# Attention and a four-expert mixture in one kernel: row loads held by GpSimd copies, one mask tile, a gate ring of two, and a refitted order

## The chip, the cores and the metric

The kernel runs on one core of a Trainium2 chip. A core has a matrix engine (TensorE, PE in the profile; its weight loads are shown apart as PEld), a vector engine (VectorE, DVE), an activation engine (ScalarE, ACT), GpSimd (POOL) and a sync engine (SyncE, SP) that here only issues DMAs. GpSimd too issues DMAs. Engines run their own queues in order and wait for each other by semaphores. The metric is the device time of one execution in microseconds, as the median of several runs.

## What is computed

Four batches of attention with 8 heads, 768 positions and head size 64. Each position sees the first 4 positions (the sinks) and the last 128 (the window). The result is laid out as 3072 tokens of 512 features and goes through four experts, each two matrix products with a ReLU between; the experts' outputs are summed with weights that are normalised per token.

```python
keep = is_sink | in_window                       # first 4 keys, or 0 <= q-k < 128
a = softmax(where(keep, q @ k.T / 8, -1e9))
x = (a @ v)                                      # as (3072, 512)
p = domain_probs / (domain_probs.sum(-1) + 1e-9)
out = sum_e p[:, e] * (relu(x @ w1[e]) @ w2[e])  # w1: 512x1024, w2: 1024x512
```

## The kernel before

Tokens are taken in pairs of 128-row blocks: three pairs in each of four batches, named (b, g). Attention of a batch makes the rows x of its three pairs; the mixture turns each pair, for each expert e, into a "unit" (b, g, e): first layer, ReLU and gate, second layer.

**Attention.** q and k rows come as tiles `qkn` by cast loads on GpSimd's DMA queue (`load_nat`, L248), v as `vx` (`load_v`, L316). For batch 0 TensorE turns them (L605), for the later ones SP issues a DMA transpose into `qkT` (`turn_nat`, L259). `scores` (L689) makes products of 64-row tiles (L708), two heads side by side; ScalarE takes the exponential (L733) into `aT`; VectorE multiplies by a 0/1 mask (L727 for both heads of a later batch, L742 for one head of batch 0); in the first group of batch 0 the mask is instead added by a product with `ident` (L702). `values` (L751) multiplies by v (L774, and L767 for the sinks); then normalisation (L801 to L819), and a DMA transpose of `onat` into `xT` (L791). `sinks` (L669) holds the scores of the first four keys, on 32-column tiles. For the sinks of group 1 in a batch from 1 on, all row blocks that they cover must be turned.

**Mixture.** The first layer is either plain (L1118) or "fast": a seven-product scheme on 2x2 blocks (P1 to P7) whose additions VectorE and ScalarE do. Fast units come in two forms. In the gated form (`emit_fast`, L1182; products L1208) VectorE multiplies with a gate row that was spread over all partitions: `gates`, 128 KB per unit, loaded by SP from a DRAM tile `gate_rows` (`load_gate`, L471, DMA L478). In the turned form (`emit_turning`, L1285; products L1320) the token is on the partition, the gate is a column of `own_gates`, and the result X goes through a DMA transpose (L1301) into H; X needs two free half tiles for each unit, kept in the list `resting`. The second layer of most pairs is a chain of seven products (L1493) on H and on sums S0, S1 that VectorE makes (`chore`, L1434 and L1411); of the first two pairs it is plain (L1579) with the gate applied at L1589 and L1591 into `osbw`.

**Order.** The kernel plans itself while it is built. Lines 118 to 229 keep a clock for every engine and for two DMA queues; each recorded instruction advances them by an estimated cost (`act`, `dve`, `pool`, `lands`, `sp`). `later(engine, ready, slack, run)` puts work of VectorE and ScalarE on a list; `flush` records the piece that is due first. The main loop (L1662) records, at each step, the PE work of lowest priority number that is ready (scores, values, a first-layer product, a second-layer product); numbers such as DUE, LEAD, SHARE_OF, FORM and MASK set these priorities. So constants move instructions on every engine. Loads stand in the list `loads` and are recorded when the plan says that their buffer is free; at run time GpSimd issues them in this order as soon as the semaphores allow, which can be earlier or later than planned. `held` (L1703) is a two-element GpSimd copy of `qkT` after the last transposes of batches 1 and 2: GpSimd issues nothing that stands behind it until these have landed.

The gate tiles form a ring of four (`NGATE = 4`): the load for unit n may go when unit n-4 is done.

Of the kernel before, what the change touches and what calls it, by code (L numbers as in the profile page):

```python
# [16 lines left out]
def kernel(  # L17
# [46 lines left out]
    EXPERTS = {(1, 0): (0, 2, 1, 3), (1, 1): (3, 2, 1, 0), (1, 2): (3, 2, 1, 0), (2, 2): (2, 0, 3, 1), (3, 1): (3, 2, 1, 0)}  # L64
# [7 lines left out]
    LOW_SECOND = 2.7  # L72
    HIGH_PRODUCT = 1.9
    EARLY = -0.01
    MASK = 5000
    GATE = 800
    GATE0 = 300
    FORM = 6000
    TOKEN = 3000
    MARGIN = 500  # L80
    HOLD = 0
    FULL = 7
    STEP0 = 0.03
    READY = 40
    REST = 3000
    LANDS = 0
    SCALED = 300
    SHARED = 2
    MARGIN1, MARGIN2 = 4000, 14000
    OWNED_READ = 152  # L90
    WIDE = 2
    OPEN = 2.5
    SOON = 34000
# [6 lines left out]
    ONE = 2  # L100
    HOLDS = 2
    MORE = 2
    BOTH = 1
    PAIR = 0
    OVER = 4
    ALONE = 2.0
    BEHIND = 1500
    CHORES = 3
    BIASED = 1
# [349 lines left out]

    gate_sb = {}  # L460
    gate_tiles = [consts.tile([P, 2, 2, P], FP32, name=f"gates{i}") for i in range(NGATE // 2)]

# [8 lines left out]
    def load_gate(pair, e):  # L471

        i = len(gate_sb) % NGATE
        x = gate_tiles[i // 2][:, i % 2]
        if FIRST <= len(gate_sb) < NGATE:
            nc.vector.memset(x[0:1, 0, 0:1], 0.0)
            dve(1, fixed=150)
        nc.sync.dma_start(  # L478
            out=x.rearrange("p t n -> p (t n)"), in_=gate_rows[pair, e].rearrange("t n -> (t n)").partition_broadcast(P),
        )  # L480
        gate_sb[pair, e] = x
        sp(takes=300)

# [26 lines left out]
    for tb in (2, 3):  # L510
# [18 lines left out]
    LOW = 32768.0  # L529
    low = [lent[:, 5 * P:8 * P], lent[:, 8 * P:12 * P]]  # L530
    nc.vector.tensor_scalar(
        out=low[0].rearrange("p (n q) -> p n q", n=3)[:, 0::2], in0=two, scalar1=LOW, scalar2=-LOW, op0=ALU.mult, op1=ALU.add,
    )
    nc.vector.tensor_scalar(out=low[0][:, P:2 * P], in0=own, scalar1=-LOW, scalar2=None, op0=ALU.mult)
    nc.vector.memset(low[0][0:NSINK, 0:2 * P], 0.0)
# [3 lines left out]
    x = low[1].rearrange("p (n c q) -> p n c q", n=2, c=2)  # L539
    nc.scalar.activation(out=x[:, :, 0], in_=two, func=AF.Copy, scale=-LOW)  # L540
    nc.scalar.activation(out=x[:, :, 1], in_=two, func=AF.Copy, scale=LOW, bias=-LOW)
    mask0 = consts.tile([P, 3 * P], BF16, name="mask0")
    mask1 = consts.tile([P, 4 * P], BF16, name="mask1")
    made = []

    def make_mask(i):
        def run(engine):
            x = (mask0, mask1)[i]
            if i:
                nc.scalar.activation(out=x, in_=low[i], func=AF.Copy, scale=1 / LOW, bias=1.0)  # L550
                act(4 * P)
            else:
                nc.vector.tensor_scalar(out=x, in0=low[i], scalar1=1 / LOW, scalar2=1.0, op0=ALU.mult, op1=ALU.add)
                dve(3 * P)
            made.append(i)
        later(("dve", "act")[i], (24000.0, 11700.0)[i], 8000, run)
# [132 lines left out]
    def scores(b, hp, g, more=False):  # L689
# [10 lines left out]
        if biased:  # L700
            for ph in range(2):
                nc.tensor.matmul(sps[ph][:, 0:w], lhsT=ident, rhs=low[min(g, 1)], start=True, stop=False, skip_group_check=True)  # L702
            pe(2 * w, ready, n=2)
# [18 lines left out]
        if b == 0:  # L722
            part = join(2, masked)
        else:
            def mask_both(at):
                def run(engine):
                    nc.vector.tensor_mul(a, a, m[:, None, :].to_broadcast([P, 2, w]))  # L727
                    masked(dve(2 * w, rate=1.92))
                later("dve", at, MASK, run)
            part = join(2, mask_both)  # L730
        for ph in range(2):
            def run(engine, ph=ph):
# [8 lines left out]
                def mask_one(engine):  # L741
                    nc.vector.tensor_mul(a[:, ph], a[:, ph], m)  # L742
                    part(dve(w, rate=1.92))
# [216 lines left out]
    class Mixture:  # L960


        def __init__(self):
# [13 lines left out]
            mine = [u for u in self.order if u[0] >= OWN]  # L977
            self.turning = set(mine[TURNED_UNITS[0]:len(mine) - TURNED_UNITS[1]])
# [46 lines left out]
        def opened(self, b, g, e):  # L1025
# [11 lines left out]
            def complete(at):  # L1037
                self.H_at[b, g, e] = at
                self.finished.add((b, g, e))
                if (b, g) >= PAIRS[0]:  # L1040
                    self.waiting.append((b, g, e))
                    load_gates()
                    if not TURNED_UNITS[1] and self.gated[-1] == (b, g, e):
                        self.rest_gates()
# [39 lines left out]
        def emit_first(self, what, ready):  # L1084
# [56 lines left out]
            def run(engine):  # L1141
# [5 lines left out]
                part(at)  # L1147
            later("dve", end, GATE0, run)

# [32 lines left out]
        def emit_fast(self, u, m, ready):  # L1182
# [40 lines left out]
            def gated(dst, src, half_, ready, slack, slot=None, then=None):  # L1223
# [16 lines left out]
                def run(engine):  # L1240
# [44 lines left out]
        def emit_turning(self, u, m, ready):  # L1285
# [47 lines left out]
            def gated(k, s, src, ready, slack, slot=None, then=None):  # L1333
                gate = own_gates[:, 2 * ((b - OWN) * NG + g) + s, e:e + 1]

                def run(engine):
                    if engine == "act":
                        nc.scalar.activation(out=src, in_=src, func=AF.Relu)  # L1338

                        def scaled(engine):  # L1340
                            nc.scalar.mul(X[k][:, :, s], src, gate)  # L1341
                            done(act(n))
# [3 lines left out]
                    done(dve(n, fixed=OWNED_READ))  # L1346

                def done(at):
                    if slot is not None:
                        take(slot, at)  # L1350
# [40 lines left out]
        def chore(self):  # L1391
# [40 lines left out]
            def form(engine):  # L1432
                x = steps.pop(0)
                x[0](*x[1:])  # L1434
                at = dve(QF * P, self.stored[-1] if (b, g) == PAIRS[0] else 0.0, rate=1.92)
                if steps:
                    go(form, self.until(b, g, e, "P6 P7".split()[len(steps) == 2]))
# [128 lines left out]
        def emit_second(self):  # L1566
# [20 lines left out]
            def run(engine):  # L1587
                if e == 0:
                    nc.vector.tensor_scalar(out=dst, in0=op, scalar1=sc, scalar2=None, op0=ALU.mult)  # L1589
                else:  # L1590
                    nc.vector.scalar_tensor_tensor(  # L1591
                        out=dst, in0=op, scalar=sc, in1=dst, op0=ALU.mult, op1=ALU.add,
                    )
# [5 lines left out]
            later("dve", end, 400, run)  # L1599
            self.since = 0  # L1600
# [36 lines left out]
    work = [sum(NFB * NDB * G * (1 if (b, g) < START[e] else 7 / 8) + NFB * NDB * G * (1 if (b, g) < PAIRS[0] else 7 / 8) for g in range(NG) for e in range(E)) for b in range(B)]  # L1637
    ahead, upto, loaded, wide, rowed = 0, 0.0, 0, 0, 0
    asked = []
# [22 lines left out]
    while mix.more() or att.more():  # L1662
# [28 lines left out]
        if x and t["pool"] < now + 1500 and free_ring(x):  # L1691
            loads.remove(x)
            x[0](*x[1:])
        if turns and (ahead < 2 or not mix.second) and landed.get(("qk", *turns[0]), 1e12) < now and (turns[0][0] <= ahead or turns[0][0] == ahead + 1 and not att.todo):
# [7 lines left out]
            if 0 < b < B - 1 and x[1] == NQB - 1:  # L1702
                nc.gpsimd.tensor_copy(out=held, in_=qkT[b][:, 1, NHP - 1, S - 2:S])  # L1703
                pool(2, turned_at[x])
                nat_loads(b + 1, range(NQB))
                turns += [(b + 1, tb) for tb in range(NQB)]
        flush(now)
        mix.tokens()
# [3 lines left out]
        if ahead + 1 < B and not att.more() and (ahead == 0 or (ahead + 1, 0) in turned_at) and (ahead == 0 or mix.done >= sum(work[:ahead]) * LEAD[ahead - 1]):  # L1712
            ahead += 1
            if ahead == 1:
                own_load()
            elif ahead == 2:
                own_made()
            att = Attention(ahead)
# [79 lines left out]
```

## Time and profile before

| what | value |
|---|---|
| median of 3 runs | 354.05 us (353.97 to 354.15) |
| span of the profiled execution | 351.9 us |
| first matmul / start of the last | 1.4 us / 348.5 us |
| PE, PEld, DVE, ACT, POOL busy | 346.2, 266.0, 282.8, 208.3, 71.6 us |
| matmuls | 3721 |
| granted TensorE clock | 1.000 |
| gate loads (L478) | 20 of 128 KB |
| DMA transposes | 67 |

The profile gives the profiled execution by its span, from its first instruction to its last; the runs' time is 2.15 us longer. Times inside the profile count from the start of the span. The chain of waits is followed back from the last instruction: each piece says what the next one had to wait for. A matmul's duration contains its way through the array, so its pace is read from many in a row. In the stage table the two numbers after a stage are its length and PE's busy time; the number behind x is a count.

### The profile page before, as it was taken

How to read it: one execution, taken by the hardware profiler on the slowest of the kernel's cores; microseconds unless marked ns; L12 is line 12 of the kernel's file. 1: busy time of each engine (PE TensorE's matmuls, PEld its weight loads, DVE VectorE, ACT ScalarE, POOL GpSimd, SP SyncE). 2: the span in 40 equal slices, each digit the busy share in tenths (PEclk: the TensorE clock that was granted, in tenths of full speed). 3: DMA queues.
4: the chain of work that ended last, by engine and by line, in shares of the span. 5: the costliest groups of instructions: out<-in, count | busy, mean ns of one | idle time of the engine just before them, and what ended most of it. 6: DMA issues, size and time to landing. Idle time of an engine off the chain costs nothing.

```text
span 351.9 us, 9351 instructions
## 1 busy us (share of the span) xinstructions
PE 346.2 (98%) x3721; PEld 266.0 (76%) x3721; DVE 282.8 (80%) x672; ACT 208.3 (59%) x476; POOL 71.6 (20%) x89
## 2 busy tenths in 40 slices
PE   8999999999999999999999999999999999999996
PEld 3685769656789998998999886755856676666685
DVE  5886999878999999799898999578768586675740
ACT  6863624447874443647453539689589767666611
POOL 8946114330546206100152000000000000000000
PEclk9999999999999999999999999999999999999999
DMA  9999999999999999920999602545437733545441
GB/s 178 178 188 195 223 214 181 179 160 174 162 147 165 121 145 122 132 64 9 109 173 159 113 32 62 120 101 120 80 91 174 127 89 93 120 120 115 67 120 61
DMA packets 161032, 45.61 MB, mean 130 GB/s; under 512 B 144740, under 2 KB 156996, under 8 KB 160988
## 3 DMA queue, kind: packets, MB, share of 16 engines
q0 software_dynamic: 79104, 17.31, 56.4%
q1 hardware_dynamic: 80828, 27.18, 40.1%
q8 instruction: 29, 0.48, 0.5%
q10 hardware_dynamic: 1056, 0.52, 0.5%
q14 instruction: 15, 0.12, 0.1%
HBM read 38.39 MB, written 6.34 MB: 127 GB/s over the span
## 4 chain that ended last, share of the span: by engine, by line
PE 75%; DMA 19%; POOL 5%; issue 1%; ACT 0%; POOLq 0%; SPq 0%
PE acc L1493 35%; PE cps L1320 17%; PE cps L1208 15%; DMA w<-in_moe_w_dram 12%; DMA qkn<-in_k_dram 4%; DMA qkT<-qkn 3%; PE sps L708 3%; PE od L774 2%; POOL qkn L251 2%; POOL w L331 1%; POOL vx L318 1%; PE hps L1118 1%; PE od L767 1%; POOL w L341 0%; PE acc L1579 0%
## 5 line engine op out<-in xcount | busy, mean ns | idle before, releaser
L1493 PEld LDWEIGHTS <-H 128*128 128x128 bf16 x708 | 66.5, 98 | 17.9 <-issue 1.1
L1493 PE MATMUL acc<-w,H 128*128 128x256 bf16 x420 | 56.9, 273 | 0.0
L733 ACT ACTIVATE aT<-sps 128x512 bf16<-128x512 f32 (+1 forms) x96 | 47.2, 579 | 16.3 <-PE sps L708 16.2
L1208 PEld LDWEIGHTS <-w 128*128 128x128 bf16 x640 | 39.1, 98 | 1.2 <-issue 0.5
L1493 PEld LDWEIGHTS <-S 128*128 128x128 bf16 x320 | 30.3, 98 | 9.5 <-issue 0.8
L1241 DVE SCALAR_TENSOR_TENSOR H<-cps,gates 128x512 bf16<-128x512 f32 x54 | 36.6, 683 | 0.0
L1338 ACT ACTIVATE cps<-cps 128x512 f32<-128x512 f32 x44 | 25.5, 585 | 17.5 <-PE cps L1320 17.0
L1118 PE MATMUL hps<-xT,w 128*128 128x256 bf16 x256 | 31.9, 273 | 0.1
L819 ACT ACTIVATE onat<-od,R 128x64 bf16<-128x64 f32 x108 | 24.9, 324 | 11.4 <-DVE R L801 11.1
L318 POOL DMA_DIRECT2D vx<-in_v_dram x24 | 21.4, 903 | 43.0 <-PE od L774 31.2
L1208 PEld LDWEIGHTS <-vf 128*128 128x128 bf16 x480 | 29.3, 98 | 1.0 <-issue 0.5
L1579 PE MATMUL acc<-w,H 128*128 128x512 bf16 x128 | 29.9, 379 | 0.0
L1493 PE MATMUL acc<-wf,H 128*128 128x256 bf16 (+1 forms) x216 | 29.6, 272 | 0.0
L1118 PEld LDWEIGHTS <-w 128*128 128x128 bf16 x256 | 24.1, 98 | 4.7 <-issue 0.9
L1341 ACT ACTIVATE rest<-cps,own_gates 128x512 bf16<-128x512 f32 x37 | 25.5, 693 | 0.7
L727 DVE TENSOR_TENSOR aT<-aT,mask 128x1024 bf16<-128x1024 bf16 (+1 forms) x36 | 22.7, 640 | 3.1 <-ACT aT L733 2.8
L251 POOL DMA_DIRECT2D qkn<-in_q_dram x22 | 19.7, 896 | 23.3 <-DMA qkT<-qkn 14.7
L1208 PE MATMUL cps<-T,w 128*128 128x128 bf16 x320 | 24.3, 219 | 0.0
L1208 PE MATMUL cps<-xT,w 128*128 128x128 bf16 x320 | 24.1, 219 | 0.0
L1320 PE MATMUL cps<-w,T 128*128 128x512 bf16 x80 | 23.8, 379 | 0.0
L1320 PE MATMUL cps<-vf,T 128*128 128x512 bf16 x80 | 23.6, 379 | 0.0
L1554 ACT COPY osb<-acc 128x256 f32<-128x256 f32 x32 | 12.1, 382 | 19.3 <-PE acc L1493 19.1
(145 smaller groups left out, 673.5 us busy)
## 6 DMA issues: line engine op xcount, KB each, us to landing
w<-in_moe_w_dram POOLq DMA_DIRECT2D x6, 1024.0 KB, 18.4
out_dram<-osb SPq DMA_DIRECT2D x16, 256.0 KB
vx<-in_v_dram POOLq DMA_DIRECT2D x24, 128.0 KB, 6.5
qkn<-in_q_dram POOLq DMA_DIRECT2D x22, 128.0 KB, 6.7
qkn<-in_k_dram POOLq DMA_DIRECT2D x22, 128.0 KB, 7.4
gates<-gate_rows SPq DMA_DIRECT2D x20, 128.0 KB
w<-in_moe_w_dram POOLq DMA_DIRECT2D x4, 256.0 KB, 6.9
w<-in_moe_w_dram POOLq DMA_DIRECT2D x2, 512.0 KB, 11.5
```

The costliest lines, as they stand in the source:

```text
L251: nc.gpsimd.dma_start(out=both[:, i], in_=src[b, :, tb * P:(tb + 1) * P, :].rearrange("h p d -> p h d"),)
L318: nc.gpsimd.dma_start(out=vx[tb][:, :, 0:D], in_=v[b, :, tb * P:(tb + 1) * P, :].rearrange("h p d -> p h d"),)
L733: nc.scalar.activation(out=a[:, ph], in_=sps[ph][:, 0:w], func=AF.Exp, scale=scale)
L819: nc.scalar.mul(o[:, qi, hp, ph * D:(ph + 1) * D], od[:, qi, ph, 0:D], R[:, qi, ph])
L1118: nc.tensor.matmul(h[:, i].rearrange("p (q n) -> p q n", q=2), lhsT=w1_sb[e][:, db, fb * P:(fb + 1) * P], rhs=xT[b, g][:, :, db], start=(i ...
L1208: nc.tensor.matmul(y[:, f], lhsT=A[:, d, f * P:(f + 1) * P], rhs=T[:, d], start=(m in ("P1", "P5") and f == 0 and d == 0), stop=(d == 1), ...
L1241: nc.vector.scalar_tensor_tensor(out=dst, in0=src, scalar=0.0, in1=gate, op0=ALU.max, op1=ALU.mult)
L1320: nc.tensor.matmul(y.rearrange("p f n -> p (f n)"), lhsT=T[:, d], rhs=A[:, d], start=(m in ("P1", "P5") and d == 0), stop=(d == 1), skip_g ...
L1338: nc.scalar.activation(out=src, in_=src, func=AF.Relu)
L1341: nc.scalar.mul(X[k][:, :, s], src, gate)
L1493: nc.tensor.matmul(y, lhsT=self.operand(b, g, e, m)[:, f], rhs=forms[e][m][:, f, cs], start=(k == 0 and f == 0 and m in (("P1", "P5", "P2" ...
L1579: nc.tensor.matmul(op, lhsT=H[:, fb // QF, fb % QF, s], rhs=w2_sb[e][:, fb, :], start=(fb == 0), stop=(fb == NFB - 1),)
```

## The change

- **Held row loads.** `marked` remembers the tile that VectorE last wrote by plan (a masked `aT`, an X, an S or H sum). Before each recorded q/k or v load of batches 2 and 3 (`HELD = 2`), `hold` has GpSimd copy two elements of that tile into `held`. The load, behind it in GpSimd's queue, can't go earlier. There are 24 such copies, beside the two of before.
- **One mask tile.** `masks` (four 128-column blocks) takes the place of `mask0` (three) and `mask1` (four). The column order of group 0 is changed (`GROUPS[0]`), so that the first group's mask is blocks 1 to 3 and the other groups use blocks 0 and 1 twice by broadcast. The second bias source `low[1]` and its two ScalarE operations are gone.
- **Gate ring of two.** `NGATE = 2`: the load for unit n goes when unit n-2 is done; the plan has a gating wait for `gate_at`, its gate's landing.
- **Turned units.** Two tiles `row0`, `row1` are in `resting` from the start (`HALVES = 2`). The turned units are the same 20 as before, now written out as a list; `own_gates` covers batches 1 to 3 instead of 2 and 3 (72 columns instead of 48), and is normalised 26 us of plan after its load.
- **First pairs' scaling.** The scaling for e = 0 (four of them) goes from VectorE to ScalarE.
- **Costs and constants.** The plan's costs of ScalarE, VectorE and loads are changed, and most of the constants; experts' order within a pair is changed. The built program has the same products; one more dummy matmul stands in the head (26 for 25).

```diff
-        [(0, 0, 2), (1, 1, 1)],
+        [(1, 1, 1), (0, 0, 2)],
...
-    NGATE = 4
+    NGATE = 2
-    OWN = 2
-    TURNED_UNITS = (4, 0)
+    OWN = 1
+    TURNED_UNITS = (0, 0, ..., 1, 1)
-    MIX = 6
-    SHARE_OF = (1.01, 0.92, 0.96)
-    LEAD = (1.01, 0.99)
-    DUE = 1.9
+    MIX = 9
+    SHARE_OF = (0.92, 0.89, 0.95)
+    LEAD = (1.005, 0.97)
+    DUE = 1.6
-    MASK = 5000
-    GATE = 800
-    FORM = 6000
+    MASK = 8500
+    GATE = 300
+    FORM = 3500
-    LANDS = 0
+    LANDS = -1400
+    HALVES = 2
+    HELD = 2
+    GATE_LANDS = 600
...
-        t["act"] = at + max(196, 68 + cols / 1.23)
-        return at + max(350, 205 + cols / 1.2)
+        t["act"] = at + max(200, 76 + cols / 1.23)
+        return at + max(375, 230 + cols / 1.2)
-        t["dve"] = at + fixed - 85 + cols / rate
-        return at + fixed + 35 + cols / rate
+        t["dve"] = at + fixed - 77 + cols / rate
+        return at + fixed + 60 + cols / rate
+    mark = []
+    def marked(at, x):
+        mark[:] = [at, x]
+    def hold():
+        nc.gpsimd.tensor_copy(out=held, in_=mark[1])
+        pool(2, mark[0])
-        at = max(t["sw"], issued + 1500)
+        at = max(t["sw"], issued + 800)
...
         gate_sb[pair, e] = x
-        sp(takes=300)
+        gate_at[pair, e] = sp(takes=300) + GATE_LANDS
...
-            later("dve", end, GATE0, run)
+            later("dve", max(end, gate_at[b * NG + g, e]), GATE0, run)
...
-                later("dve", ready, slack, run)
+                later("dve", max(ready, gate_at[b * NG + g, e]), slack, run)
...
-            self.G, self.resting = {}, []
+            self.G = {}
+            self.resting = [(0.0, mo.tile([P, QF, 2, P], BF16, name=f"row{i}", tag=f"row{i}", bufs=1)) for i in range(HALVES)]
...
                 if e == 0:
-                    nc.vector.tensor_scalar(out=dst, in0=op, scalar1=sc, scalar2=None, op0=ALU.mult)
+                    nc.scalar.mul(dst, op, sc)
...
             loads.remove(x)
+            if x[0] is not load_w1 and x[0] is not load_w2 and x[1] >= HELD:
+                hold()
             x[0](*x[1:])
```

More of the change, by code (lines that the diff above doesn't have):

```diff
@@ L100 @@
     ONE = 2
-    HOLDS = 2
+    HOLDS = 3
     MORE = 2
@@ L104 @@
     PAIR = 0
[L105 to L108, printed above, removed]
+    OVER = 5
+    ALONE = 0.3
+    BEHIND = 2400
+    CHORES = 5
     BIASED = 1
@@ L529 @@
     LOW = 32768.0
-    low = [lent[:, 5 * P:8 * P], lent[:, 8 * P:12 * P]]
+    low = lent[:, 5 * P:8 * P]
     nc.vector.tensor_scalar(
-        out=low[0].rearrange("p (n q) -> p n q", n=3)[:, 0::2], in0=two, scalar1=LOW, scalar2=-LOW, op0=ALU.mult, op1=ALU.add,
+        out=low.rearrange("p (n q) -> p n q", n=3)[:, 0:2], in0=two, scalar1=LOW, scalar2=-LOW, op0=ALU.mult, op1=ALU.add,
     )
-    nc.vector.tensor_scalar(out=low[0][:, P:2 * P], in0=own, scalar1=-LOW, scalar2=None, op0=ALU.mult)
-    nc.vector.memset(low[0][0:NSINK, 0:2 * P], 0.0)
+    nc.vector.tensor_scalar(out=low[:, 2 * P:], in0=own, scalar1=-LOW, scalar2=None, op0=ALU.mult)
+    nc.vector.memset(low[0:NSINK, P:], 0.0)
     nc.vector.reduce_sum(
@@ L538 @@
     )
[L539 to L543, printed above, removed]
+    masks = consts.tile([P, 4 * P], BF16, name="masks")
+    mask0, mask1 = masks[:, P:], masks[:, 0:2 * P]
     made = []
@@ L547, in run @@
         def run(engine):
-            x = (mask0, mask1)[i]
             if i:
-                nc.scalar.activation(out=x, in_=low[i], func=AF.Copy, scale=1 / LOW, bias=1.0)
-                act(4 * P)
-            else:
-                nc.vector.tensor_scalar(out=x, in0=low[i], scalar1=1 / LOW, scalar2=1.0, op0=ALU.mult, op1=ALU.add)
-                dve(3 * P)
+                nc.scalar.activation(out=masks[:, 0:P], in_=own, func=AF.Copy, scale=-1.0, bias=1.0)
+                nc.scalar.copy(out=masks[:, P:2 * P], in_=own)
+                act(P)
+                act(P)
+            else:
+                nc.vector.tensor_scalar(out=masks[:, 2 * P:], in0=low[:, P:], scalar1=1 / LOW, scalar2=1.0, op0=ALU.mult, op1=ALU.add)
+                dve(2 * P)
             made.append(i)
@@ L701, in scores @@
             for ph in range(2):
-                nc.tensor.matmul(sps[ph][:, 0:w], lhsT=ident, rhs=low[min(g, 1)], start=True, stop=False, skip_group_check=True)
+                nc.tensor.matmul(sps[ph][:, 0:w], lhsT=ident, rhs=low, start=True, stop=False, skip_group_check=True)
             pe(2 * w, ready, n=2)
@@ L726, in run @@
                 def run(engine):
-                    nc.vector.tensor_mul(a, a, m[:, None, :].to_broadcast([P, 2, w]))
-                    masked(dve(2 * w, rate=1.92))
+                    x = a if g == 0 else a.rearrange("p h (r c) -> p (h r) c", r=2)
+                    nc.vector.tensor_mul(x, x, m[:, None, :].to_broadcast([P, 2 if g == 0 else 4, w if g == 0 else 2 * P]))
+                    at = dve(2 * w, rate=1.92)
+                    marked(at, a[:, 1, w - 2:w])
+                    masked(at)
                 later("dve", at, MASK, run)
@@ L1042, in complete @@
                     load_gates()
-                    if not TURNED_UNITS[1] and self.gated[-1] == (b, g, e):
+                    if self.gated[-1] == (b, g, e):
                         self.rest_gates()
@@ L1345, in run @@
                     nc.vector.tensor_scalar(out=X[k][:, :, s], in0=src, scalar1=0.0, scalar2=gate, op0=ALU.max, op1=ALU.mult)
-                    done(dve(n, fixed=OWNED_READ))
+                    done(dve(n, fixed=OWNED_READ) if slot is not None else dve(n, rate=1.92, fixed=214))
                 def done(at):
+                    marked(at, X[k][:, 0, s, 0:2])
                     if slot is not None:
@@ L1435, in form @@
                 at = dve(QF * P, self.stored[-1] if (b, g) == PAIRS[0] else 0.0, rate=1.92)
+                marked(at, x[1][:, 0, 0:2])
                 if steps:
@@ L1588, in run @@
                 if e == 0:
-                    nc.vector.tensor_scalar(out=dst, in0=op, scalar1=sc, scalar2=None, op0=ALU.mult)
[L1590 to L1593, printed above, removed]
+                    nc.scalar.mul(dst, op, sc)
+                    acc_free[bank] = act(Dout)
+                    return
+                nc.vector.scalar_tensor_tensor(
+                    out=dst, in0=op, scalar=sc, in1=dst, op0=ALU.mult, op1=ALU.add,
+                )
                 acc_free[bank] = at = dve(Dout, fixed=218)
@@ L1598, in run @@
                     self.stored.append(sp(at))
-            later("dve", end, 400, run)
+            later("dve" if e else "act", end, 400, run)
             self.since = 0
@@ L1637 @@
     work = [sum(NFB * NDB * G * (1 if (b, g) < START[e] else 7 / 8) + NFB * NDB * G * (1 if (b, g) < PAIRS[0] else 7 / 8) for g in range(NG) for e in range(E)) for b in range(B)]
-    ahead, upto, loaded, wide, rowed = 0, 0.0, 0, 0, 0
+    ahead, upto, loaded, wide, rowed, owned = 0, 0.0, 0, 0, 0, 1e12
     asked = []
@@ L1706 @@
                 turns += [(b + 1, tb) for tb in range(NQB)]
+        if owned + OWNS < now:
+            owned = 1e12
+            own_made()
         flush(now)
@@ L1715 @@
                 own_load()
-            elif ahead == 2:
-                own_made()
+                owned = now
             att = Attention(ahead)
```

37 lines of the change are left out of this document (20 added, 17 removed).

## The prediction, as put on record before the changed kernel ran

> **What bounds the kernel now.** I read the page's busy shares, then the chain of waits in order of time, then the stage table, then single rows.
>
> ```profile
> span 351.9 us, 9351 instructions
> PE 346.2 (98%) x3721; PEld 266.0 (76%) x3721; DVE 282.8 (80%) x672; ACT 208.3 (59%) x476; POOL 71.6 (20%) x89
> ...
> PE 75%; DMA 19%; POOL 5%; issue 1%; ACT 0%; POOLq 0%; SPq 0%
> ```
>
> PE is nearly never idle. But a busy PE is not yet a streaming PE, so I take paces from the chain's pieces:
>
> ```profile
> 60.20 14.86 DMA qkn<-in_k_dram
> 75.11 10.75 DMA qkT<-qkn
> ...
> 117.01 2.18 PE acc L1493 x20
> ...
> 200.80 4.91 PE cps L1208 x88
> ```
>
> A 256-column matmul takes 2.18/20 = 0.109 us, a 128-column one 4.91/88 = 0.056. With the 512-column pace (0.216) and the score matmuls counted once per row-group pair, which start 3 ns apart, the 3721 matmuls stream for 334.1 us. The rest of 351.9 is: 1.4 before the first matmul, 3.4 after the start of the last, 31 visits to the row-tiled scores and sinks at 0.19 each (5.9), and waits, about 7. The 0.19 is read at one visit:
>
> ```profile
> 93.40 1.04 PE L1118 MATMUL hps<-xT,w 128*128 128x256 bf16 x8
> 94.37 0.29 PE L669 MATMUL sinks<-qkT,ksd 128*32 128x256 bf16 x4
> 94.59 0.62 PE L708 MATMUL sps<-qkT 64*128 64x128 bf16 x12
> 95.14 0.39 PE L1493 MATMUL acc<-w,H 128*128 128x256 bf16 x2
> ```
>
> The eight matmuls from 93.40 fill 8 x 0.109, to 94.27; the sinks start 0.10 late. The twelve scores stream 0.45 us, to 95.04; the next product starts 0.10 late. Of the 7 us of waits, 1.5 is the half-rate clock of the dummy matmuls before 5 us, which no order changes, and about 4 are data waits before 23 us. After 25 us only 1.17 is left: 0.37 at 86.0 (sinks behind the DMA transposes of the chain above), 0.15 and 0.12 near 241, 0.13 and 0.08 at 140, and four pieces of 0.04 to 0.14. **So PE's own work sets the end, and little idle time is left to win.** VectorE is next:
>
> ```profile
> 100.00:110.00 10.00, 10.00 (x161) 9.30 (x159) 10.00 (x25) 7.31 (x25) 3.39 (x4) 1.00 1.69 161
> 150.00:160.00 10.00, 10.00 (x150) 9.22 (x148) 9.96 (x23) 5.14 (x16) 0.00 (x0) 1.00 0.17 56
> 310.00:320.00 10.00, 10.00 (x71) 6.65 (x69) 5.57 (x13) 6.65 (x13) 0.00 (x0) 1.00 0.61 157
> ```
>
> Columns: stage, PE, PEld, DVE, ACT, POOL, clock, DMA share, GB/s. From 90 to 190 us DVE is busy 76 to 100%: a microsecond that DVE loses there is hard to make up. After 210 it has room.
>
> **The change, part by part.** Places below are PE streaming time, added up at these paces along the built program; another engine's instruction has the place of the PE instruction beside which it was recorded. Place 148.2 of before is 155.56 on the profile's clock: add about 7.
>
> *PE's own list.* The refitted order has 3722 matmuls: one more 256-column dummy in the head (+0.11). Visits to row-tiled matmuls rise from 31 to 34, because pairs of score steps are split more often: 3 x 0.19 = +0.57. Sum **+0.68**, certain, and on the path, since PE is the bound. The Trainium skill (TensorEngine Tiling (Array Packing), Key Properties) says that changing the tiling mode drains TensorE; by that rule each visit must cost, and the 0.10 on each side agrees.
>
> *Batch 1's rows.* From 12 to 86 us the chain is row and weight loads. The ring of two takes two 128 KB gate loads out of it: those issued at 37.80 and 38.28, whose packets took 1.8 us each beside other loads (42.71 to 44.53, 44.49 to 46.41). The wait of 0.37 at 86.0 needs only 0.37 of that. Between 0 and -0.37, I take **-0.3**, nearest to its being gone. Next late is PE itself.
>
> *Head and masks.* The two ScalarE operations of the second mask source (0.42 and 0.40 us at 3.8 to 4.6) go, the mask itself becomes two 128-column copies; VectorE's casts at 5.07 follow its own queue, so nothing moves. Four flips now stand ahead of a turn that waited 0.16 (12.65), and two turns are joined where one waited 0.25 (20.61). Between 0 and -0.41: **-0.15**, in the middle, as the chain through VectorE behind them is unchanged.
>
> *Later waits.* The 0.8 left after 25 us beside the 86.0 one can all go, or be replaced by others: the numbers of recorded steps with under 0.9 us from producer to PE are 31 before and 21 after (places from 30 on), a thinner list. Between -0.8 and +0.5: **-0.3**. In it lies the shift of six gatings from ScalarE (0.59 + 0.69 each) to VectorE (0.75) in the last stage, where DVE has room, and of four scalings of 0.75 from VectorE to ScalarE around 70, where ScalarE is under half busy.
>
> *Gate ring of two.* Before, a gate load was recorded at least 19 us ahead of its first use. Now the load waits until the unit two back is gated, and the 16 later ones lead by 2.0 (place 148.2 to 150.2), 4.1 (91.4), 4.7 (174.4), 5.3 (176.9), 6.3 (117.8), 6.4 (111.9), 7.4 twice, the rest 9 or more. Issue to last packet, from before's 20 gate loads: 2.4 to 3.1 in quiet stretches (152.83 to 155.38, 155.56 to 158.49), 3.8 to 8.1 beside row loads. So at 150 VectorE stops 0.5 to 1.0, at 95 up to 0.6, near 180 up to 1.0, near 124 up to 1.0. Behind that instruction stand all of VectorE's queue; PE's bank releases there have some 0.9 us of lead. PE pays 0 to 1.5 in all: **+0.3**, since the one sure late load exceeds PE's lead by about nothing to 0.4. The Trainium skill (DMA: Bandwidth & Descriptors, Anatomy of one DMA) gives 2.0 us and 0.3 for 128 KB, an estimate of 2.3 for each; by it only the 2.0 lead is short and this term is +0.1; the loads of 3.8 and more beside row loads say that it is a floor.
>
> *Held loads.* 24 copies of 128x2 join POOL's queue ahead of the row loads, each waiting for one VectorE write. The two such copies of before:
>
> ```profile
> POOL held L1703 <- DMA qkT<-qkn: 34.2, 2, 18.8
> ...
> L1703 POOL COPY held<-qkT x2: 184/212/240, 92.0 to 135.0; 128x2 bf16<-128x2 bf16 x2
> ```
>
> 24 x 0.21 = 5 us on an engine with 20% busy: covered. Queued behind each are the row loads, behind these SP's transposes and then the scores. The copies also add waits the other way: whoever next writes the marked tile waits for POOL. The closest are ScalarE's exponentials at places 90.1 and 92.3, 7.4 and 6.3 us after their copies; POOL starts 2 to 3 us late there, as its queue is held by batch 1's transposes to 91.95. Enough cover. Contention is the other cost: 13.20 (POOL, 1.16 us) and 13.99 below.
>
> ```profile
> 13.20 1.16 POOL L647 TENSOR_TENSOR vsd<-vsf,sel 128x520 bf16<-128x520 f32 x1
> 13.99 0.52 DVE L1174 TENSOR_TENSOR T<-xT 128x256 bf16<-128x256 bf16 x1
> ```
>
> That VectorE step takes 0.28 in the median, here 0.52. The two copies at 92.0 and 135.0 lengthened nothing beside them. So each costs VectorE 0 to 0.24, 0 to 5.8 in all, and PE 0 to 0.5: **+0.1**, near the copies' own rows. The Trainium skill (SBUF — State Buffer, the shared port pair) has VectorE's two-input steps and GpSimd's reads exclude each other for a whole instruction; by it about half the copies would block VectorE, an estimate of 2.5 us of its time, and PE's part would be +0.3.
>
> Row loads now start when planned, so fewer run into transposes; their landing is not on the path unless the rival below holds: 0.
>
> **Sum**: +0.68 - 0.3 - 0.15 - 0.3 + 0.3 + 0.1 = +0.33: span 352.2. The runs' median stands 2.15 above the span (354.05 against 351.9); carried over: **354.4**, +0.1%. That counts as no change: 0.2%, 0.71 us, is about what a measurement of this kernel can tell.
>
> **Rivals.** *Batch 2's rows come late (slower).* In before, nine loads from 108.38 to 115.30 and the transposes among them hamper each other:
>
> ```profile
> 118.25 0.32 SPq L478 DMA_DIRECT2D gates<-gate_rows  x1
> ...
> 121.57 12.03 SPq L263 DMA_TRANSPOSE qkT<-qkn  x2
> 133.70 2.20 SPq L478 DMA_DIRECT2D gates<-gate_rows  x3
> ```
>
> The last row load, issued at 115.30, landed at 131.62, and the last transpose at 135.0: 19.7 us. Held loads put the last issue at place 114.9, about 122.3; with the same 19.7 they end at 142.0. Batch 2's sinks stand at place 132.9, 139.9, so PE stops 2.1; the gate loads behind these transposes (place 120.9, used at 128.3) come late too, another 0.5 to 1.5. It decides from a drain of over 17.6 us. For it: nine loads in 7.5 us of places again. Against it: an undisturbed series (92.44 to 100.92) drains in 15, and three transposes now go ahead of the loads. 354.4 + 2.1 + 1 = 357.5; a milder form, in which gate loads alone wait, gives 355.2 to 356.
>
> *The refit pays (faster).* All the wins come and no cost: 0.68 - 0.37 - 0.41 - 0.8 = -0.90, 353.15. Against it: it needs every wait gone.
>
> *The change does nothing*: +0.68 and the waits as they are but for the 86.0 one: 354.4, inside the forecast.
>
> **Chances.** Forecast (within 0.2%) 0.55; gate or row lateness beyond it 0.33, of which the full form 0.1; faster 0.12. The likeliest case's own range is 353.4 to 354.7. Leaving out half of the faster case and the full late form, the range is 353.3 to 355.9.
>
> **What would show it.** The static part: 34 visits and PE's streaming sum +0.68. Gate: VectorE waits for DMA gates near 157 and 102 on the profile's clock. Held loads: last row load of batch 2 issued near 122, landing by 132, and PE's sinks near 140 without a DMA wait. The 86.0 wait gone. I am wrong if PE waits over 1 us after 90, or if VectorE's two-input steps beside the copies are longer by 0.2.

## The result, and the profile after

| kernel | median (range) | runs | before, beside it | ratio, 95% interval |
|---|---|---|---|---|
| changed kernel | 358.88 us (358.45 to 359.25) | 4 | 354.09 | 1.0138 [1.0121, 1.0154] |
| the same, run again | 358.97 us (358.36 to 359.41) | 4 | 353.77 | 1.0143 [1.0128, 1.0158] |

The change makes the kernel 1.4% slower. 354.4 was forecast and 355.9 was the upper end of the range: the prediction was wrong. The profiled execution of the changed kernel took 358.63 us. The page's span, its busy line and its chain by engine:

```profile
span 356.9 us, 9383 instructions
...
PE 348.1 (98%) x3722; PEld 266.2 (75%) x3722; DVE 284.0 (80%) x677; ACT 200.8 (56%) x462; POOL 78.6 (22%) x113
...
PE 60%; DMA 23%; DVE 9%; POOL 5%; issue 2%; ACT 0%; POOLq 0%; DVEq 0%; SPq 0%
```

PE's busy share is 98% as before, and tells nothing. The chain tells it: PE's part fell from 75% to 60%, and VectorE, which was not in it at all, has 9%. The chain's long pieces (start, us, what):

```profile
60.56 15.16 DMA qkn<-in_k_dram
75.78 10.85 DMA qkT<-qkn
...
99.05 5.14 DMA gates<-gate_rows
...
130.02 4.24 DMA gates<-gate_rows
...
158.62 3.12 DMA gates<-gate_rows
...
186.80 4.41 DMA gates<-gate_rows
```

The first two pieces are the rows of batch 1, as before. The other four are new: gate loads, the shortest of which takes 3.12 us from its issue to its landing (the last update of the semaphore that the gating waits for). The stage table at the stages that were shown of before (stage, PE, PEld, DVE, ACT, POOL, clock, DMA share, GB/s):

```profile
100.00:110.00 10.00, 9.41 (x126) 8.42 (x125) 8.72 (x21) 5.08 (x16) 3.15 (x5) 1.00 0.87 76
150.00:160.00 10.00, 10.00 (x172) 9.80 (x170) 8.71 (x16) 4.66 (x12) 0.00 (x0) 1.00 0.46 72
310.00:320.00 10.00, 10.00 (x72) 6.84 (x71) 7.25 (x19) 6.61 (x11) 0.00 (x0) 1.00 0.46 88
```

In 100 to 110 VectorE went from 10.00 busy to 8.72, and PE from 10.00 to 9.41: idle time has come where VectorE had none to give. Here is one of the four places in the chain of waits, piece by piece:

```profile
158.01 0.59 DVE H L1256
158.60 0.02 issue
158.62 3.12 DMA gates<-gate_rows
161.74 0.03 issue
161.77 0.02 DVEq L1256
161.79 0.04 issue
161.83 0.70 DVE H L1256
162.53 0.04 issue
162.58 0.22 PE od L781
```

A gating ends, which frees the buffer; the load goes 0.02 us later; it is there at 161.74; the next gating can start, and PE, which waits for VectorE's queue behind it, goes on at 162.58. (L1256 is the gating that was L1241 before.) The same from VectorE and PE, with the wait in brackets:

```profile
159.10 0.69 DVE L1276 TENSOR_TENSOR cps<-H,cps 128x512 f32<-128x512 f32 x1
161.83 0.69 DVE L1256 SCALAR_TENSOR_TENSOR H<-cps,gates 128x512 bf16<-128x512 f32 x1 [2.04 <-DMA gates<-gate_rows]
...
161.03 0.61 PE L1223 MATMUL cps<-T,w 128*128 128x128 bf16 x8
162.58 0.22 PE L781 MATMUL od<-vsd,sinkA 128*128 128x130 bf16 x1 [0.94 <-DVE H L1256]
```

VectorE's waits for gates over the whole kernel (us in total, times, longest), in both profiles of the changed kernel; the one of 2.0 is the one above:

```profile
DVE H L1256 <- DMA gates<-gate_rows: 4.3, 4, 2.0
```

```profile
DVE H L1256 <- DMA gates<-gate_rows: 4.8, 4, 1.8
```

The stops stand at 104, 134, 162 and 191 us: 0.96, 0.78, 2.04 and 0.55 in the first profile, 0.76, 1.28, 1.82 and 0.94 in the second. PE's waits behind them are 3.6 us in the first; in the same stretch of before, PE waited some 0.3. Four theories were tried. **Ring**: a load that may go only when the unit two back is gated has too short a lead (the time from the gating that frees its buffer to the gating that needs it); VectorE stops and PE follows. **Order**: the refitted order is worse whatever the ring. **Copies**: the 24 GpSimd copies cost VectorE or delay the loads. **Head**: 0.84 us for first-layer weights at 18 us, new in the first profile.

### The profile page after: what moved, and what is told of

The parts are those of the page before. It is cut to its first block, busy times and chain, and to the rows that moved or that the text cites. A ratio compares the mean times of both kernels' runs of the same rounds, so it can differ in the third digit from the quotient of the medians.

```text
span 356.9 us, 9383 instructions
## 1 busy us (share of the span) xinstructions
PE 348.1 (98%) x3722; PEld 266.2 (75%) x3722; DVE 284.0 (80%) x677; ACT 200.8 (56%) x462; POOL 78.6 (22%) x113
## 4 chain that ended last, share of the span: by engine, by line
PE 60%; DMA 23%; DVE 9%; POOL 5%; issue 2%; ACT 0%; POOLq 0%; DVEq 0%; SPq 0%
PE acc L1510 30%; PE cps L1335 17%; DMA qkn<-in_q_dram 11%; PE cps L1223 7%; DMA gates<-gate_rows 5%; DVE H L1256 5%; DMA qkn<-in_k_dram 4%; DMA qkT<-qkn 3%; PE sps L718 2%; POOL qkn L263 2%; PE od L788 2%; DVE H L1291 1%; POOL vx L330 1%; DVE cps L1276 1%; POOL w L343 1%
## 5 line engine op out<-in xcount | busy, mean ns | idle before, releaser
L1510 PEld LDWEIGHTS <-H 128*128 128x128 bf16 x732 | 68.2, 98 | 18.2 <-issue 1.7
L1510 PE MATMUL acc<-w,H 128*128 128x256 bf16 x432 | 57.8, 273 | 0.0
L1256 DVE SCALAR_TENSOR_TENSOR H<-cps,gates 128x512 bf16<-128x512 f32 x54 | 36.0, 683 | 4.6 <-DMA gates<-gate_rows 4.3
L1353 ACT ACTIVATE cps<-cps 128x512 f32<-128x512 f32 x38 | 22.0, 586 | 14.3 <-PE cps L1335 14.2
L1335 PE MATMUL cps<-w,xT 128*128 128x512 bf16 x80 | 23.6, 379 | 0.0
L738 DVE TENSOR_TENSOR aT<-aT,masks 128x1024 bf16<-128x1024 bf16 (+1 forms) x36 | 22.5, 640 | 1.2 <-ACT aT L746 0.9
L1223 PE MATMUL cps<-T,vf 128*128 128x128 bf16 x320 | 22.9, 219 | 0.0
```

Source lines behind the costliest of these rows:

```text
L738: nc.vector.tensor_mul(x, x, m[:, None, :].to_broadcast([P, 2 if g == 0 else 4, w if g == 0 else 2 * P]))
L1223: nc.tensor.matmul(y[:, f], lhsT=A[:, d, f * P:(f + 1) * P], rhs=T[:, d], start=(m in ("P1", "P5") and f == 0 and d == 0), stop=(d == 1), ...
L1256: nc.vector.scalar_tensor_tensor(out=dst, in0=src, scalar=0.0, in1=gate, op0=ALU.max, op1=ALU.mult)
L1335: nc.tensor.matmul(y.rearrange("p f n -> p (f n)"), lhsT=T[:, d], rhs=A[:, d], start=(m in ("P1", "P5") and d == 0), stop=(d == 1), skip_g ...
L1510: nc.tensor.matmul(y, lhsT=self.operand(b, g, e, m)[:, f], rhs=forms[e][m][:, f, cs], start=(k == 0 and f == 0 and m in (("P1", "P5", "P2" ...
```

## The experiments

All of them compute the whole result. Some 22 matmul records are missing in most of these traces (3699 of 3722), so a single gap of 0.1 or 0.2 us between equal matmuls is no wait; the waits named below have a releaser. "Before" is always as measured beside the kernel in question.

**Four buffers, loads at the same places.** The two added buffers lie in a tile that is free until the turned units.

```diff
-        i = len(gate_sb) % NGATE
-        x = gate_tiles[i // 2][:, i % 2]
+        i = len(gate_sb) % 4
+        x = (gate_tiles[0] if i < 2 else mix.row0.rearrange("p f t n -> p (f t n)").bitcast(FP32).rearrange("p (i t n) -> p i t n", i=2, t=2))[:, i % 2]
...
```

> The changed kernel with its gate loads in four buffers instead of two (the two added ones lie in a tile that the turned units take up only later). Every instruction of every engine stands at the same place of its queue; only the wait of a gate load for the gating two units back is gone, so a load goes as soon as SP comes to it. Theory ring (a gate load that may go only when the unit two back is gated has a shorter lead than its way to the landing; VectorE stops in its queue and TensorE follows): the four VectorE stops for gates (0.96, 0.78, 2.04 and 0.55 us) and TensorE's waits behind them (3.6 us) go, 355.2 us, between 354.8 and 356. Theory order (the refitted order is worse whatever the ring): 358.9, within 0.5. Theory copies (the GpSimd copies cost VectorE): 358.9 too.

Measured: 355.68 us (355.05 to 356.85), ratio 1.0045 [1.0031, 1.0059]. The ring's wait alone, with every instruction at its place, carries 3.2 of the 4.8 us. Its profiled execution was its slowest, and shows the second part. VectorE and SP:

```profile
133.79 1.29 DVE L1257 SCALAR_TENSOR_TENSOR H<-cps,gates 128x512 bf16<-128x512 f32 x2 [1.28 <-DMA gates<-gate_rows]
...
128.13 1.24 SPq L275 DMA_TRANSPOSE qkT<-qkn  x1
129.41 0.57 SPq L490 DMA_DIRECT2D gates<-gate_rows  x1
```

No buffer was wanted there: the load stood in SP's queue behind a transpose that waited for its rows until 128.13.

**The changed kernel without copies**, twice. Only `hold`'s copy is left out; the plan's charge for it stays.

```diff
     def hold():
-        nc.gpsimd.tensor_copy(out=held, in_=mark[1])
         pool(2, mark[0])
```

> The changed kernel without the 24 GpSimd copies ahead of the row loads of batches 2 and 3; all other instructions at the same places of their queues. Theory copies (they lengthen VectorE's steps, or delay the loads that they hold): at least 0.5 us faster, 358.4 or less. Theory ring and theory order: 358.9 within 0.5; slower if the loads, now free to go early, run into transposes and gate loads, up to 360.

> The changed kernel without copies once more, in more rounds, since its first four times spread from 356.61 to 359.64 and leave open whether the copies cost anything where the ring is two. With early gate loads they cost nothing (355.3 with, 355.4 without). Theory copies through the ring: without them the row loads start and land earlier, gate loads beside them get shorter ways, 357.3 within 0.4. If that first result was spread: 358.9 within 0.4.

Measured: 357.33 us (356.61 to 359.64), ratio 1.0109 [1.0074, 1.0144]; again 357.64 (356.55 to 358.51), 1.0104 [1.0086, 1.0123], below the interval of the changed kernel run again. So the copies do cost about 1.3 us here (358.97 - 357.64). What both profiles share is the stop at 104: without copies the seven row loads from 93 to 99 are issued sooner (the last at 98.21 and 98.35 instead of 99.54 and 99.38), the gate load behind them lands 4.2 to 4.4 us after its issue instead of 4.9 to 5.1, and the stop is 0.20 us in the first profile and gone in the second. Lined up matmul by matmul with the changed kernel run again, PE gains 0.6 and 0.7 us there. The rest lies in the other stops, which differ from profile to profile, and was not taken apart. The waits for gates of the second profile are three:

```profile
DVE H L1255 <- DMA gates<-gate_rows: 3.9, 3, 2.1
```

**Before with a ring of two**, and nothing else of the change; the plan's clocks advance as with four.

```diff
...
-            len(gate_sb) < (NGATE if t["pe"] > GATED else FIRST) or mix.gated[len(gate_sb) - NGATE] in mix.finished
+            len(gate_sb) < (2 if t["pe"] > GATED else FIRST) or mix.gated[len(gate_sb) - 2] in mix.finished
...
-        i = len(gate_sb) % NGATE
-        x = gate_tiles[i // 2][:, i % 2]
+        i = len(gate_sb) % 2
+        x = gate_tiles[0][:, i]
...
```

> The kernel before with a gate ring of two buffers instead of four, and nothing else of the change: the order on TensorE, VectorE, ScalarE and GpSimd is that of before (without two adds of a one-time set-up), only SP's gate loads stand later. Their leads by place, from issue to first use, are 3.6, 4.2, 5.7 us for the three shortest and 7.7 or more for the others; the one of 3.6 stands behind the 12 us of transposes that SP sits in from 121.6 to 133.6 us in before, and its gating then comes at about 136 instead of 129. Theory ring: TensorE waits 4 to 7 us in all, 358 to 361 us. Theory order: 354.1 within 0.5, as the order is that of before.

Measured: 360.49 us (359.95 to 361.02), ratio 1.0187 [1.017, 1.0203]: 6.6 us, in the old order. The ring alone makes the kernel slow, and the order that it was fitted with softens it. Its one large stop, on VectorE and SP:

```profile
135.99 0.69 DVE L1248 SCALAR_TENSOR_TENSOR H<-cps,gates 128x512 bf16<-128x512 f32 x1 [5.98 <-DMA gates<-gate_rows]
...
118.58 0.53 SPq L486 DMA_DIRECT2D gates<-gate_rows  x1
...
121.66 9.43 SPq L263 DMA_TRANSPOSE qkT<-qkn  x2
131.60 0.80 SPq L486 DMA_DIRECT2D gates<-gate_rows  x2
```

PE waited 5.8 us behind these 5.98: nearly all of it passes through. More came behind it. The mean granted TensorE clock from 139 to 143 is 0.57 (it is 1.00 before and behind), and lined up matmul by matmul with before, PE falls another 1.5 us back there. All four runs have a granted clock under 1 (0.990 to 0.995). Both profiles of the changed kernel have 1.000, so this part of the 6.6 us is none of its loss.

**The plan knows what frees the buffer.**

```diff
-        gate_at[pair, e] = sp(takes=300) + GATE_LANDS
+        gate_at[pair, e] = sp(t["dve"], takes=300) + GATE_LANDS
```

> The changed kernel, but its plan is told that a gate load starts no earlier than the gating that frees its buffer; in the changed kernel the plan lets it start whenever SP's own clock allows, in four cases before the gating that releases it. The order comes out anew (3725 matmuls, 35 visits to the row-tiled ones, streaming time 0.65 us above that of the changed kernel), with a shortest lead of 3.1 us where it was 2.0. Theory ring, with the plan's blindness as the reason for the short leads: most of the 3.6 us of gate waits go and 0.65 to 0.85 of streaming comes, 355.7 to 357.5 us. Theory order: 358.9 or more.

Measured: 361.63 us (360.95 to 361.72), ratio 1.0215 [1.02, 1.023]. No theory had this. The gate load of the new order that was issued at 120.72 was on the chain for 7.43 us, beside batch 2's row loads; the gating behind it:

```profile
128.25 1.29 DVE L1256 SCALAR_TENSOR_TENSOR H<-cps,gates 128x512 bf16<-128x512 f32 x2 [2.65 <-DMA gates<-gate_rows]
```

PE lost 2.7 us there in three waits. VectorE's waits for gates are 3.8 us in all, no more than in the changed kernel (4.3 and 4.8), so they are not what makes this run slower than that one. Its own list, reckoned 0.65 longer with one visit more, is a part. Another is the clock: its mean from 129 to 134 is 0.66, and the three runs with a granted clock of 0.994 or 0.995 took 361.59 to 361.72, the one with 1.000 took 360.95. Knowing when a load starts does not help a plan that has it land 0.6 us later.

**The changed kernel again.**

> The changed kernel once more, on the chip and in the call of the next three. In the two runs that share its head (four buffers; no copies) the wait of 0.84 us for first-layer weights at 18 us was 0.17. Theory head (that wait belongs to the execution that was profiled, not to the order): it is under 0.3 here and the time still 358.9 within 0.5, since it does not carry the loss. Were it systematic, 0.8 again. The four VectorE stops for gates come again at 104, 134, 161 and 191 us, 3 to 5 us in all.

Measured: 358.97 us; the wait of 0.84 is 0.18, and the stops come at the same four places. **Head** falls: that wait belonged to one execution, and the time is the same without it.

**Early loads.** Four buffers, and loads issued where a ring of four allows them (leads of 16 us of place or more); the plan still reckons with the ring of two.

```diff
...
+        while len(gate_sb) < len(mix.gated) and (
+            len(gate_sb) < (4 if t["pe"] > GATED else FIRST) or mix.gated[len(gate_sb) - 4] in mix.finished
+        ):
+            b, g, e = mix.gated[len(gate_sb)]
+            load_gate(b * NG + g, e)
...
```

> The changed kernel with four gate buffers, and its gate loads issued where a ring of four allows it (16 us of place or more ahead of use) instead of where the ring of two does; the plan still reckons with the loads of two, so TensorE, ScalarE and GpSimd keep the order of the changed kernel, and VectorE too. The run with four buffers but late places kept one stop of 1.3 us at 134.5, for a gate load that stood in SP's queue behind a transpose waiting for its rows. Theory ring, with SP's queue as its second part: that stop goes too, no VectorE wait for gates is left, 354.3 to 355.0 us. Theory order: what is left over the kernel before (355.7 against 353.9) is the refit's; 355.7 within 0.3.

Measured: 355.31 us (355.15 to 355.37), ratio 1.004 [1.0025, 1.0055], above the ring's forecast and just under the order's. VectorE waits for no gate any more: lined up matmul by matmul with the second profile of the changed kernel, PE gains 0.29 + 0.43 + 1.32 + 0.13 + 0.89 + 0.36 + 0.76 = 4.18 us from 105 to 195. But it loses 0.68 at 87, where PE's waits show:

```profile
PE sinks L687 <- DMA qkT<-qkn: 1.2, 1, 1.2
```

It was 0.2 and 0.5 in the two profiles of the changed kernel: the ring of two keeps two gate loads out of batch 1's row series.

**Early loads without copies.** The last kernel without `hold`'s copy.

> The last one without the 24 GpSimd copies, everything else in the same order. The changed kernel without copies was 1.5 us faster than with them, in a profile in which the gate stops had shrunk too. Theory copies by themselves (they lengthen VectorE's or hold back the loads): another 0.5 us or more off. Theory copies through the ring (without copies the row loads land at other times, so that the short gate loads beside them do too): within 0.3 of the run with early loads and copies, as no gate load is short here.

Measured: 355.42 us (355.24 to 355.69), ratio 1.0042 [1.0025, 1.0059]. **Before with copies**, at the same places in its order:

```diff
...
             loads.remove(x)
+            if x[0] is not load_w1 and x[0] is not load_w2 and x[1] >= 2:
+                nc.gpsimd.tensor_copy(out=held, in_=mark[0])
             x[0](*x[1:])
```

> The kernel before with the 24 copies and nothing else of the change; all other instructions at the same places (the plan is not told of the copies). Theory copies by themselves: 0.5 us or more slower, 354.4 or above. Theory copies through the ring: 353.9 within 0.3, as the gate loads of before lead by 19 us or more.

Measured: 354.1 us (353.76 to 354.26), ratio 1.0006 [0.9997, 1.0015]. Both say the same: by themselves the copies cost nothing that shows. They cost through the ring alone.

**Before with two gate loads later**, after batch 1's transposes instead of among its row loads.

```diff
+    ROWS_IN = 88000
...
+        while len(gate_sb) < len(charged) and (not 4 <= len(gate_sb) < 6 or t["pe"] > ROWS_IN):
...
```

> The kernel before, with the fifth and sixth of its 20 gate loads issued after batch 1's transposes instead of among its row loads (the two that the ring of two takes out of that series in the changed kernel come earlier there; the plan reckons as before, so every other instruction keeps its place; the two loads still lead their use by 14.9 and 22.3 us of place). TensorE's wait for batch 1's transposes was 0.37 us in before; with early loads in the changed order it was 1.26 against 0.24 to 0.59 with the ring of two. If the gate loads in the row series cost the rows time, the wait of 0.37 goes: 353.4, within 0.2 of it, faster than before by about 0.1%. If the rows' time does not depend on them: 353.8 and the wait stays.

Measured: 353.53 us (353.29 to 353.95, 11 runs), ratio 0.9989 [0.998, 0.9998]. PE no longer waits for the transposes. This is the one version that beats both kernels, by 0.1%.

**Early loads but for two**: before 86 us the gate loads of the changed kernel, after it those of a ring of four.

```diff
...
+        while len(gate_sb) < len(charged) or t["pe"] > ROWS_IN and len(gate_sb) < len(mix.gated) and mix.gated[len(gate_sb) - 4] in mix.finished:
...
```

> The run with early loads again, but with its third to sixth gate load where the changed kernel has its third and fourth, and its fifth and sixth after batch 1's transposes: before 86 us the same gate loads go as in the changed kernel, after it as with a ring of four. Accounting so far: early loads 355.3, of which 1.26 us was the wait for batch 1's transposes. If that wait came from the two gate loads more in the row series, it is 0.3 to 0.6 here, 354.4 to 354.7, and what is left over the kernel before is the list's 0.65. If the wait is the refit's own (rows ordered later): 355.3.

Measured: 354.71 us (354.36 to 354.95, 11 runs), ratio 1.0022 [1.0013, 1.0031]. PE's wait for the transposes and the page's chain by engine:

```profile
PE sinks L690 <- DMA qkT<-qkn: 0.4, 1, 0.4
```

```profile
PE 74%; DMA 22%; POOL 2%; issue 1%; SPq 0%; ACTq 0%; ACT 0%; POOLq 0%
```

VectorE is off the chain, as in before. Of 358.9 us, 4.2 were the ring's; 0.86 is left over 353.85, 0.69 of it the list (below), and **order** as the main cause falls. The one mask tile, the scaling on ScalarE, the turned units and the copies are all in this run, so together they are none of the 4.2. What makes the last 0.2 was not taken apart.

**The plan knows a landing of 5 us** as well as what frees the buffer; the ring stays at two.

```diff
-    GATE_LANDS = 600
+    GATE_LANDS = 5000
...
-        gate_at[pair, e] = sp(takes=300) + GATE_LANDS
+        gate_at[pair, e] = sp(t["dve"], takes=300) + GATE_LANDS
```

> The changed kernel with its ring of two, but a plan that knows both what frees the buffer (the gating two units back) and that a load takes 5 us after it, where the changed kernel reckons with 0.6. The order comes out anew: shortest lead 7.2 us where it was 2.0; streaming time 0.22 us more and 36 visits instead of 34 (0.4). The run whose plan knew the first and not the second had a lead of 3.1 to 4 us at five loads and stopped up to 2.6 us for one that took 7.4 us. Theory ring, by the lead: gate waits under 0.5 us, 355.0 to 356.0. If two buffers are too few whatever the lead: 358 or more.

Measured: 358.5 us (358.26 to 359.21), ratio 1.0132 [1.0117, 1.0146]. VectorE waits for no gate, so the lead was mended, and yet nothing is won. Two stages of it:

```profile
120.00:130.00 10.00, 9.81 (x157) 9.46 (x155) 8.46 (x19) 2.68 (x5) 5.30 (x8) 1.00 2.07 180
130.00:140.00 10.00, 8.33 (x99) 6.16 (x99) 9.93 (x26) 6.36 (x23) 0.59 (x2) 1.00 1.08 144
```

With its gatings planned later, VectorE has idle time before 130 (8.46 of 10; the run with early loads but for two has 9.83), and PE waits 2.5 us between 129 and 136, most of it for what VectorE then does late. The list itself was reckoned 0.6 us longer (0.22 of streaming and two visits more). How much better a plan made for two buffers could be stays open.

## Why the prediction was wrong

The step that failed is **"Gate ring of two ... PE pays 0 to 1.5 in all: +0.3"**. Its mechanism and its places were right (VectorE stops for gates at 104 and 162 us, where 102 and 157 were named, and near the two others); the term was 4.2 us, by the run with early loads but for two against the changed kernel. Four things made it small:

- *The lead was counted in PE's place.* It is the time from the gating that frees the buffer to the next gating that needs it, both on VectorE. At place 148.2 the lead of 2.0 was 1.17 us on the clock: issue at 158.62, and VectorE done with the instruction before at 159.79. The wait was 2.04, where 0.5 to 1.0 was said. All four together were 4.3 and 4.8, where the stated parts add up to 3.6 at most.
- *The landing was read too short.* The 2.4 to 3.1 and 3.8 to 8.1 us are times to a load's last packet. VectorE waits for the semaphore, and by its updates in the trace of before the same loads landed 2.85 us (152.83) and 3.40 us (155.56) after their issue, those beside row loads 4.2 to 8.6. The load at 158.62 in the changed kernel took 3.12.
- *PE's 0.9 us of lead was taken off.* From 90 to 150 VectorE is 89 to 100% busy in the run with early loads but for two, and has nothing to catch up with: its 5.98 us in before with a ring of two cost PE 5.8, its 4.8 us in the changed kernel 4.18. Only at 162 did much of PE's lead hold: in the second profile VectorE's 1.82 us there became 0.89 + 0.36 of PE's.
- *A queue behind the wait.* The load at 130.02 stood behind a transpose that waited for rows, the milder form of the first rival. It was priced as a rival, when it belonged in the sum.

Point by point:

- *PE's own list, +0.68*: 34 visits as forecast. The tiling changes 75 times where it did 69 times, at 0.096 us each in the mean of those with no wait beside them: 0.58, and with the dummy's 0.11, 0.69. The term was right.
- *Batch 1's rows, -0.3*: the two loads do cost the rows time. The transpose that the sinks wait for lands at 85.86 us in before and at 84.53 in before with two later; in the changed order it lands at 87.08 with early loads and at 86.60 with early loads but for two. But the new order issues the row load on the chain later (at 60.56 and 60.31 in the changed kernel, at 60.20 in before); its rows land at 86.64 and 86.47, and a wait of 0.2 to 0.5 is left. In all about 0.
- *Head, -0.15*: not to be told from the spread. The first product behind the turned x starts at 22.3 us in the profile of before, at 23.0 in before with two later, at 23.3 and 22.8 in those of the changed kernel.
- *Later waits, -0.3*: the two near 241 are gone; one of 0.1 near 270 is new.
- *Held copies, +0.1 (0 to 0.5)*: nothing by themselves, about 1.3 with the ring of two. I asked what they do to VectorE, not what later row loads do to the gate load behind them.

```profile
L211 POOL COPY held<-H 128x2 bf16<-128x2 bf16 x9 | 3.5, 394 | 16.5 <-DVE H L1450 16.4
L211 POOL COPY held<-aT 128x2 bf16<-128x2 bf16 x8 | 2.3, 293 | 7.8 <-DVE aT L738 7.7
L211 POOL COPY held<-S 128x2 bf16<-128x2 bf16 x7 | 1.7, 237 | 23.7 <-DVE S L1450 23.7
```

These are the copies in the changed kernel (busy us, mean ns of one): it is they that are longer than the 212 ns in before, not VectorE's steps. VectorE's busy time is 283.7 us with copies and 283.8 without (the two runs with early loads). The Trainium skill (SBUF — State Buffer, the shared port pair) has the loser block for a whole instruction; the estimate of 2.5 us of VectorE time from it is not borne out here.

The rivals: the full form of late rows did not come (last row load of batch 2 issued at 124.78, no wait at its sinks). Faster did not come, and the change did not do nothing. None had the ring as the main term, since its bound of 1.5 was taken as an end: the price of a wait on an engine with no slack is nearly its whole length, four times over (4.18 of 4.8 us).

## What to carry to other kernels

When a buffer ring shrinks, take each load's lead from the end of the step that frees the buffer to the start of the step that needs it, on the engine that does both, and set against it the slowest landing that the trace shows at that place, to the semaphore and not to the last packet, with what stands ahead of it in its queue. If that engine is as busy as VectorE here (89 to 100%), charge nearly all of the shortfall to the engine that follows it. Two harmless changes can be costly together: the copies and the ring each need the run without the other.

## What was not expected of the hardware

- The same 128 KB gate load took from 2.84 us (issued at 157.96 in the first profile without copies, in a quiet stretch) to 8.08 us (issued at 119.72 there, beside row loads) from issue to landing, by the chain. The Trainium skill (DMA: Bandwidth & Descriptors, Anatomy of one DMA) has some 2.0 us fixed for a DMA that GpSimd issues and a part by size, 2.3 for 128 KB, an estimate. SP issues these loads, and none of the 20 in the trace of before landed in under 2.8 us.
- A stop of TensorE can cost more than its length. Behind the 5.8 us in before with a ring of two, the granted clock was 0.57 in the mean from 139 to 143; behind the 2.7 us in three waits of the run whose plan knows what frees the buffer, 0.66 from 129 to 134. With 2.5 us in five waits, in the run whose plan knows a landing of 5 us, it stayed at 1.00. What decides between the last two was not tried.
- With transfers on the path the runs spread: 356.55 to 358.51 and 356.61 to 359.64 without copies, 355.15 to 355.37 with early loads.
